# An FNet and feed-forward kernel: the first roots moved from GpSimd to VectorE and ScalarE, and a new table of positions

## The chip, the cores and the metric

The kernel runs on one core of a Trainium2 chip. The metric is the device time of one execution in microseconds. The engines are named as in the profile: PE is TensorE (matmuls; PEld is its weight load), DVE is VectorE, ACT is ScalarE, POOL is GpSimd, and SP is SyncE, which only issues transfers here. POOL issues transfers too.

## The reference

```python
a = jnp.einsum("bsd,ed->bse", x, dft_hid_re)
b = jnp.einsum("bsd,ed->bse", x, dft_hid_im)
y = jnp.einsum("ts,bse->bte", dft_seq_re, a) - jnp.einsum("ts,bse->bte", dft_seq_im, b)
...
h  = x + _A_ref(_layernorm(x), dft_seq_re, dft_seq_im, dft_hid_re, dft_hid_im)
h2 = h + silu(_layernorm(h) @ w1) @ w2
```

x has 2048 rows (S) of 512 columns (D); the sequence matrices are 2048 x 2048, the hidden ones 512 x 512, w1 is 512 x 1792 and w2 1792 x 512. All is fp32.

## The kernel before

**Arithmetic.** Every fp32 operand is split into a rounded high part and a remainder, the low part, and each product is three matmuls (function `three`, L329 to L331: high by high, high by low, low by high). The split takes one pass on ACT (`rounded`, L270; for X and S tiles L421, L449, L456) and one on DVE (L274 or L276, L427). The large products are built by a Strassen-like scheme of seven products (numbers 1 to 7 in the code), so DVE also forms sums and differences of the operands before a product and of the results after it.

**Stages.** `plain(0, 0)` multiplies the normalized x by the first quarter of the sequence matrices while x is still being loaded and normalized; `fast(1, 0)` does the next quarter; `mix_fast(0)` multiplies by the hidden matrices and adds x; then `fast(0, 1)`, `fast(1, 1)` and `mix_fast(1)` do the other half of the output columns; `up` and `down`, twice, are the feed-forward part. Beside them run the normalization of h, the sums of w1, w2 and of the hidden matrices, and stores of half results to DRAM and fetches back.

**Normalizing x.** For each pair of row tiles `stats_x` takes means and variances on DVE (L370, L371); `roots_x` starts the inverse root with a square root on ACT (L291) and computes -var/2; its second half takes a reciprocal on DVE (L298) and does one Newton step and the bias; `norm_x` applies scale and bias on ACT (L403) and rounds (L421); `rest` makes the low parts on DVE (L427). With one column (one row tile) the Newton step and the bias are on DVE (L321, L325, L384) and -var/2 on ACT (L293); with two columns all of that is on POOL (L295, L302 to L305, L386, L387).

**What sets the order.** `program` creates 1598 pieces of work. `step` advances a planned clock by 0.2265 us (`MM_US`) for each matmul and gives each piece before or after it a planned time relative to it; `at` gives a planned time outright. The table `MOVED` then adds a correction to the time of piece n, and the pieces are sorted:

```python
return sorted(((t + MOVED.get(n, 0.0), at, n, f) for t, at, n, f in events), key=lambda v: v[:3])
```

They are issued in that order, and every engine, and every transfer queue, keeps it: an instruction that waits holds up all later ones of its engine. The planned times serve for the order alone; nothing waits for a clock. Most tiles lie in 51 pages of on-chip memory, which are assigned in the same order (`Plan.places`), so a transfer into a page also waits for the last use of what lay there before.

The pieces that the prediction speaks of:

- 5, 11, 12, 14: square root, rest of the root, normalizing and low parts of the second row tile.
- 16, 20, 21: statistics and root; rest of the root and normalizing; low parts, of row tiles 2 and 3 (the rest of the first group of rows).
- 23, 27: roundings of sequence tiles for the steps after that.
- 56, 57 and 102, 103, 104: root, normalizing and low parts of later pairs of row tiles; PE needs 57 for the step near 37 us and 103 for the step near 52 us.
- 72, 112: negated copies of sequence tiles (ACT, L634). 74, 189: roundings for the step near 43 us.
- 62, 115, 142, 158: sums of results of `plain` (DVE, L591, L594).
- 144, 164, 168, 277, 281, 607, 627, 637, 645: remainders (low parts) of sequence tiles; 146, 151: of X tiles; 231, 237: of the hidden matrices.
- 165, 169: transfers on POOL that add a sequence tile to one on chip (L640); 232: a store on POOL.
- 774, 801: fetches of rounded hidden matrices (SP, L854); 919: a fetch of the normalized h; 780, 910, 1001, 1025: loads of x, w2, w1 and w1 (SP); 1002: the rounding of what 1001 loads (ACT, L1074); 951: a copy of a result by ACT (L1104).
- 1267, 1489, 1583, 1587: the last adds and stores of the output (L1251, L1217).

Of the kernel before, what the change touches and what calls it, by code (L numbers as in the profile page):

```python
# [251 lines left out]
def program(nc, page, keep, small, psum, dram, x, xT, seq, hid, ffn, out):  # L252
# [33 lines left out]
    upper = keep.tile([P, 1], F32, name="upper")  # L286
    lower = keep.tile([P, 1], F32, name="lower")

    def rsqrt(var, v, t, q):

        nc.scalar.activation(q, var, AF.Sqrt, scale=1.0, bias=upper)  # L291
        if var.shape[-1] == 1:
# [81 lines left out]
    def roots_x(jj):  # L374

        done, mv, w = stats.pop(jj)
        n = len(done)
# [1044 lines left out]
```

## Time and profile before

| | us |
|---|---|
| median of 3 runs | 674.59 (673.58 to 675.31) |
| the profiled execution | 682.51 |
| its span, first to last instruction | 680.7 |
| PE busy | 664.3 (98%) |
| DVE busy | 574.5 (84%) |
| ACT busy | 374.1 (55%) |
| POOL busy | 123.4 (18%) |

In the groups and the timeline a row has the start, the duration, the engine, the line, the operation, written tile <- read tiles, the shape, and in brackets how long the engine was idle before it and what ended that. In the waits a row has who waited <- for whom, the total, how often, and the longest. In the table of stretches a row has the stretch, its length, the busy time of PE, PEld, DVE, ACT and POOL, the granted PE clock, the share of the transfer engines' time, and GB/s. The profiled execution is 7.9 us longer than the median of the runs.

### The profile page before, as it was taken

Reading aid. Unit: us, or ns where it says so; the run is one execution under the profiler, and the core shown is the slowest. Engines: PE = TensorE matmul, PEld = TensorE weight load, DVE = VectorE, ACT = ScalarE, POOL = GpSimd, SP = SyncE. Lnnn points to the kernel's source line nnn. Section 1 sums busy time; section 2 is a strip of 40 time slices with the busy share of each in tenths; the row PEclk is TensorE's granted clock in tenths of the full one; section 3 lists DMA queues with packets and bytes.
Section 4 is the critical chain, followed back from the end, with each engine's and each line's share of the span. In section 5 each row is a group of like instructions: output and inputs, shape, how many; then the busy total and the mean of one; then the engine's idle time right before and its main releaser. Section 6 shows DMA issues by size and latency. Waiting matters only on the chain.

```text
span 680.7 us, 8334 instructions
## 1 busy us (share of the span) xinstructions
PE 664.3 (98%) x2880; PEld 540.9 (79%) x2880; DVE 574.5 (84%) x714; ACT 374.1 (55%) x479; POOL 123.4 (18%) x183
## 2 busy tenths in 40 slices
PE   8999989999999999999998998999999999999997
PEld 5776868888888888878887886888888888888885
DVE  7888888998989999799999897989999753669774
ACT  5989546655454444446563744668643645655510
POOL 2562211112002331310231003426001000000000
PEclk9999989999999999999999998999999999999999
DMA  9967989999999778999999984787979725468913
GB/s 322 393 119 155 252 291 404 319 282 317 327 314 342 240 213 237 321 372 296 307 352 421 344 286 173 275 300 262 393 215 402 281 83 210 140 224 284 316 40 154
DMA packets 60425, 186.82 MB, mean 274 GB/s; under 512 B 6880, under 2 KB 13920, under 8 KB 60384
## 3 DMA queue, kind: packets, MB, share of 16 engines
q1 hardware_dynamic: 45312, 132.27, 54.8%
q0 software_dynamic: 14784, 53.77, 26.2%
q8 instruction: 22, 0.36, 0.2%
q10 hardware_dynamic: 288, 0.26, 0.1%
q14 instruction: 19, 0.16, 0.1%
HBM read 140.39 MB, written 44.32 MB: 271 GB/s over the span
## 4 chain that ended last, share of the span: by engine, by line
PE 43%; DMA 4%; DVE 3%; ACT 1%; issue 1%; SPq 0%; ACTq 0%; DVEq 0%
PE f L331 6%; PE f L329 6%; PE f L330 6%; PE y L329 5%; PE y L331 5%; PE y L330 5%; PE vx L331 3%; PE vx L329 3%; PE vx L330 3%; DMA hf<-fd 2%; DMA u<-in_ffn 2%; DVE pl L274 1%; DVE raw L742 1%; DVE pl L276 0%; ACT ph L270 0%
## 5 line engine op out<-in xcount | busy, mean ns | idle before, releaser
L270 ACT ACTIVATE ph<-raw 128x1024 fp32r<-128x1024 f32 x98 | 101.3, 1055 | 79.8 <-DVE pl L274 19.3
L274 DVE TENSOR_TENSOR pl<-raw,ph 128x1024 fp32r<-128x1024 f32 x86 | 104.3, 1233 | 15.6 <-ACT ph L270 12.7
L330 PE MATMUL m<-pl,S 128*128 128x512 f32 x192 | 75.2, 392 | 0.2
L331 PE MATMUL m<-ph,S 128*128 128x512 f32 x192 | 74.8, 389 | 0.0
L329 PE MATMUL m<-ph,S 128*128 128x512 f32 x192 | 74.7, 389 | 0.0
L329 PE MATMUL f<-gth,wf 128*128 128x512 f32 x161 | 62.6, 389 | 0.0
L330 PE MATMUL f<-gtl,wf 128*128 128x512 f32 x161 | 62.6, 389 | 0.0
L331 PE MATMUL f<-gth,wf 128*128 128x512 f32 x161 | 62.6, 389 | 0.0
L274 DVE TENSOR_TENSOR gtl<-g,gth 128x1024 fp32r<-128x1024 f32 x42 | 50.4, 1219 | 14.2 <-ACT gth L270 14.2
L270 ACT ACTIVATE gth<-g 128x1024 fp32r<-128x1024 f32 x42 | 42.6, 1053 | 33.1 <-DVE g L1236 17.2
L330 PE MATMUL m<-pl,X 128*128 128x512 f32 x144 | 56.8, 394 | 1.9 <-DVE pl L274 1.8
L329 PE MATMUL m<-ph,X 128*128 128x512 f32 x144 | 56.7, 394 | 0.0
L331 PE MATMUL m<-ph,X 128*128 128x512 f32 x144 | 56.7, 394 | 0.0
L742 DVE TENSOR_TENSOR raw<-raw,raw 128x1024 f32<-128x1024 f32 x36 | 45.8, 1275 | 0.3
L329 PE MATMUL y<-ph,hf 128*128 128x512 f32 x112 | 43.7, 390 | 1.8 <-DMA hf<-fd 1.8
L331 PE MATMUL y<-ph,hf 128*128 128x512 f32 x112 | 43.6, 389 | 0.0
L330 PE MATMUL y<-pl,hf 128*128 128x512 f32 x112 | 43.6, 389 | 0.0
L330 PEld LDWEIGHTS m<-pl,S 128*128 128x128 f32 x192 | 36.0, 188 | 9.3 <-DVE pl L274 1.7
L329 PEld LDWEIGHTS m<-ph,S 128*128 128x128 f32 x192 | 36.0, 188 | 7.5
L331 PEld LDWEIGHTS m<-ph,S 128*128 128x128 f32 x192 | 36.0, 188 | 7.4
L1107 DVE TENSOR_TENSOR g<-vx,g 128x512 f32<-128x512 f32 x28 | 19.3, 689 | 25.8 <-PE vx L331 13.5
L330 PEld LDWEIGHTS f<-gtl,wf 128*128 128x128 f32 x161 | 30.2, 188 | 6.3
(416 smaller groups left out, 1580.5 us busy)
## 6 DMA issues: line engine op xcount, KB each, us to landing
raw<-in_seq SPq DMA_DIRECT2D x83, 512.0 KB, 7.1
hf<-fd SPq DMA_DIRECT2D x28, 512.0 KB, 7.2
wf<-wd SPq DMA_DIRECT2D x28, 512.0 KB, 6.1
wf<-wd SPq DMA_DIRECT2D x28, 384.0 KB, 4.4
sf<-sd SPq DMA_DIRECT2D x18, 512.0 KB, 6.5
raw<-in_seq POOLq DMA_DIRECT2D x15, 512.0 KB, 8.2
fd<-hf POOLq DMA_DIRECT2D x14, 512.0 KB, 7.1
w<-in_ffn SPq DMA_DIRECT2D x23, 256.0 KB, 6.2
```

The lines of the kernel that those rows point to most:

```text
L270: nc.scalar.activation(hi, src, AF.Copy, scale=sign)
L274: nc.vector.tensor_tensor(lo, src, hi, op=ALU.subtract)
L329: nc.tensor.matmul(acc, wh, mh, start=first, stop=False, skip_group_check=on)
L330: nc.tensor.matmul(acc, wh, ml, start=False, stop=False, skip_group_check=on)
L331: nc.tensor.matmul(acc, wl, mh, start=False, stop=last, skip_group_check=on)
L742: nc.vector.tensor_tensor(o, a, b, op=ALU.subtract)
L1107: nc.vector.tensor_tensor(g[q, f][:, tau, :], src, g[q, f][:, tau, :], op=ALU.add)
```

## The change

First, `rsqrt` and `roots_x` no longer choose by the number of columns but by whether the roots belong to a later group of rows (those have a tuple as key). For the first group of rows, whose last two tiles have two columns, -var/2 goes from POOL to ACT, and the Newton step and the bias from POOL to DVE. The other six pairs stay on POOL.

```diff
-    def rsqrt(var, v, t, q):
+    def rsqrt(var, v, t, q, spare=False):
 
         nc.scalar.activation(q, var, AF.Sqrt, scale=1.0, bias=upper)
-        if var.shape[-1] == 1:
+        if not spare:
             nc.scalar.activation(t, var, AF.Identity, scale=-0.5, bias=lower)
         else:
             nc.gpsimd.tensor_scalar(t, var, -0.5, -0.5 * EPS, op0=ALU.mult, op1=ALU.add)
 
         def refine():
             nc.vector.reciprocal(q, q)
-            if var.shape[-1] == 1:
+            if not spare:
                 newton(v, t, q, q)
             else:
                 nc.gpsimd.tensor_tensor(v, q, q, op=ALU.mult)
...
-        refine = rsqrt(mv[:, :n, 1], v, t, r)
+        spare = isinstance(jj, tuple)
+        refine = rsqrt(mv[:, :n, 1], v, t, r, spare)
 
         def then():
             refine()
-            if n == 1:
+            if not spare:
                 nc.vector.scalar_tensor_tensor(b, mv[:, :n, 0], -1.0, r, op0=ALU.mult, op1=ALU.mult)
             else:
                 nc.gpsimd.tensor_tensor(b, mv[:, :n, 0], r, op=ALU.mult)
```

Second, the table `MOVED`: 534 of its 1019 entries have another value and 37 are new. The pieces named above, with the planned time that results (base time plus entry) before and after:

| piece | entry before | after | planned time before | after |
|---|---|---|---|---|
| 5 | -148.22 | -183.24 | -241.1 | -276.1 |
| 11 | -69.54 | -170.43 | -159.7 | -260.6 |
| 12 | -60.5 | -140.25 | -146.4 | -226.2 |
| 14 | -42.39 | -86.88 | -114.2 | -158.7 |
| 16 | -82.56 | -128.07 | -165.6 | -211.1 |
| 20 | -138.51 | -161.4 | -136.6 | -159.5 |
| 21 | -83.19 | -99.75 | -76.3 | -92.8 |
| 23 | -152.04 | -173.57 | -151.4 | -172.9 |
| 27 | -168.5 | -168.5 | -162.4 | -162.4 |
| 57 | -75.05 | -75.05 | -56.9 | -56.9 |
| 72 | -74.26 | -91.97 | -51.6 | -69.3 |
| 112 | -18.19 | -10.85 | 16.3 | 23.6 |
| 189, 74 | -7.95, -5.56 | the same | 19.6, 22.9 | 19.6, 22.9 |
| 115, 62 | 17.99, 18.84 | -0.81, 0.24 | 65.2, 73.7 | 46.4, 55.1 |
| 151, 146 | 3.99, 7.25 | -6.59, -3.29 | 61.2, 61.8 | 50.6, 51.2 |
| 231 | -40.84 | -35.43 | 59.0 | 64.4 |
| 144 | none | none | 59.5 | 59.5 |
| 165, 169 | none, 8.11 | 8.43, 3.17 | 58.4, 69.2 | 66.8, 64.3 |
| 232 | -39.41 | -31.37 | 60.9 | 69.0 |
| 164 | 1.29 | 2.81 | 71.7 | 73.2 |
| 142, 158 | 9.72, 3.24 | 9.72, 6.19 | 74.2, 74.4 | 74.2, 77.4 |
| 281, 277 | 1.14, 5.69 | 3.13, 2.42 | 74.7, 76.5 | 76.7, 73.2 |
| 627, 645 | 4.12, 1.8 | 7.6, 5.04 | 262.5, 268.3 | 266.0, 271.6 |
| 919, 801 | -8.57, -23.53 | -32.05, 4.29 | 341.7, 325.0 | 318.2, 352.8 |
| 774 | -1.69 | -1.69 | 333.2 | 333.2 |
| 780, 910 | 30.22, -25.24 | 20.32, -43.66 | 379.8, 382.0 | 369.9, 363.6 |
| 1001, 1025 | -8.22, -15.73 | -10.97, -55.02 | 382.8, 384.8 | 380.1, 345.6 |
| 1002, 951 | -13.83, none | -6.22, none | 385.0, 387.3 | 392.6, 387.3 |
| 1583, 1587 | 1.39, -0.02 | 49, -0.02 | 644.2, 644.8 | 691.8, 644.8 |
| 1267, 1489 | 106.65, 75.03 | 72.6, 19.98 | 668.1, 707.6 | 634.0, 652.5 |

Piece 607 keeps its place within 0.3 us; other pieces on DVE are moved ahead of it. The order of the matmuls on PE is the same before and after. On DVE about 210 of 542 pieces, on ACT 130 of 444, on SP 56 of 199 and on POOL 20 of 107 stand elsewhere relative to the rest of their queue.

226 rows, old and new, of the table MOVED are left out of this document.

## The prediction

> **What bounds the kernel now.** I read the page's busy shares first, then the waits of PE, then the timeline of PE around the longest of them.
>
> ```profile
> PE 664.3 (98%) x2880; PEld 540.9 (79%) x2880; DVE 574.5 (84%) x714; ACT 374.1 (55%) x479; POOL 123.4 (18%) x183
> ```
>
> PE is busy 98% of the span and the change leaves its instructions and their order alone, so the change can only move waits of PE. These are all of them:
>
> ```profile
> PE y L329 <- ACT g L1104: 2.5, 1, 2.5
> PE c L329 <- ACT X L421: 2.0, 2, 1.1
> PE m L330 <- DVE pl L274: 1.8, 1, 1.8
> PE y L329 <- DMA hf<-fd: 1.8, 1, 1.8
> PE c L541 <- ACT X L403: 1.6, 1, 1.6
> PE idle L1385 <- DVE upper L1378: 1.2, 1, 1.2
> PE c L545 <- DVE X L427: 0.6, 1, 0.6
> ```
>
> Without the start (1.2) they come to 10.3 us; 6.0 of it (2.0, 1.8, 1.6, 0.6) lies in the head, the first 100 us. A wait costs more than its idle time:
>
> ```profile
> 92.97 0.39 PE L329 MATMUL m<-ph,X 128*128 128x512 f32 x1
> 95.18 0.50 PE L330 MATMUL m<-pl,X 128*128 128x512 f32 x1 [1.82 <-DVE pl L274]
> 95.52 0.59 PE L331 MATMUL m<-ph,X 128*128 128x512 f32 x1
> 95.90 0.63 PE L329 MATMUL m<-ph,X 128*128 128x512 f32 x1
> 96.33 0.63 PE L330 MATMUL m<-pl,X 128*128 128x512 f32 x1
> ...
> 92.00:100.00 8.00, 6.18 (x20) 4.61 (x20) 7.12 (x7) 1.69 (x2) 1.59 (x3) 0.79 0.82 242
> 410.00:418.00 8.00, 5.53 (x18) 4.12 (x17) 5.75 (x7) 3.88 (x6) 0.00 (x0) 0.79 0.45 161
> ```
>
> After the wait at 93 the matmuls start 0.43 us apart (95.90 to 96.33) instead of the 0.2265 of the kernel's own MM_US, and the granted clock over these 8 us is 0.79 (the column before the last two): 0.21 x 8 = 1.7 us lost beside the 1.8. The wait that ends in the window 410 to 418 shows the same 0.79. So the wait at 93 is worth 3.5 us, the one at 411 4.2, and all seven about 14.
>
> The Trainium skill, page "TensorE: Matmul & The Clock Gate", section "Why this matters for your kernels", asks only for no idle gaps over about 3 us; by that rule the waits at 93 and 411 would cost their idle time alone, and the forecast below would be 1.7 us higher. Here the trace disagrees: a gap of 1.82 us halved the clock, so I price it at 3.5.
>
> **The change part by part.** The order follows from the code: a piece's planned time plus its entry of the table, sorted. Only the queues of DVE, ACT, POOL and SP change.
>
> *Roots of the first group of rows (pieces 16 and 20).* Seven POOL instructions become one Identity on ACT and four operations on DVE.
>
> ```profile
> 11.06 0.30 ACT L291 ACTIVATE rs<-mv,upper 128x2 f32<-128x2 f32 x1 [1.84 <-DVE rs L298]
> 11.26 1.99 ACT L270 ACTIVATE ph<-raw 128x1024 fp32r<-128x1024 f32 x2
> 13.15 1.08 ACT L403 ACTIVATE X<-x,rs 128x256 fp32r<-128x256 f32 x2
> ...
> 16.42 1.10 ACT L403 ACTIVATE X<-x,rs 128x256 fp32r<-128x256 f32 x2 [1.48 <-POOL rs L387]
> ...
> 37.06 0.63 ACT L421 ACTIVATE X<-xc 128x512 fp32r<-128x512 f32 x1
> 37.60 0.28 ACT L291 ACTIVATE rs<-mv,upper 128x2 f32<-128x2 f32 x1
> 37.78 1.04 ACT L634 ACTIVATE raw<-raw 128x1024 f32<-128x1024 f32 x1
> ```
>
> ```profile
> 46.24 0.55 POOL L302 TENSOR_TENSOR rs<-rs 128x2 f32<-128x2 f32 x1 [1.64 <-DVE rs L298]
> 46.86 1.06 POOL L303 TENSOR_TENSOR rs<-rs 128x2 f32<-128x2 f32 x1
> ...
> 50.88 0.22 POOL L387 TENSOR_SCALAR rs<-rs 128x2 f32<-128x2 f32 x1
> ```
>
> ```profile
> 10.94 0.13 DVE L298 RECIPROCAL rs<-rs 128x1 f32<-128x1 f32 x1
> ...
> 11.64 0.16 DVE L384 SCALAR_TENSOR_TENSOR rs<-mv,rs 128x1 f32<-128x1 f32 x1
> ...
> 72.83 1.22 DVE L274 TENSOR_TENSOR pl<-nb,ph 128x1024 fp32r<-128x1024 f32 x1
> 73.96 0.68 DVE L427 TENSOR_TENSOR X<-xc,X 128x512 fp32r<-128x512 f32 x1
> ...
> 89.18 1.22 DVE L591 TENSOR_TENSOR C<-C,Cp 128x1024 f32<-128x1024 f32 x1
> ```
>
> ACT could begin with these tiles only at 16.42, after 1.48 of waiting for POOL's last instruction. The same work for one tile took DVE 10.94 to 11.80, four instructions in 0.86; with two columns there is one more, so about 1.1. Added: 0.9 on DVE, 0.2 to 0.3 on ACT (the 0.28 row); the roots come about 2.5 us earlier. Left over on POOL: nothing waits there for the time that comes free, so that is worth nothing by itself.
>
> *The head, first wait (1.6).* On ACT, piece 12 (the second row tile, 13.15) stood behind the square root at 11.06, which waits for the statistics of two later tiles, and two roundings (1.99). Now it stands ahead of all three, and its own roots (piece 11) ahead of those statistics on DVE. Its first half is ready near 10.6 instead of 13.7, before PE is done with its first half-step at about 12.0. What is late next are its low parts (piece 14), about 0.5. Worth 1.1 to 1.6, I take 1.5. *Second wait (0.6).* Piece 21 stands ahead of one pair of statistics now, but PE arrives 1.5 earlier: the 0.6 stays.
>
> *Third wait (ACT X L421, the first of two, near 37).* Piece 57 ends at 37.69 in the rows. The 1.04 of piece 72 (37.78) moves from behind it to ahead of it; what ACT idled for earlier POOL roots in this stretch is saved in exchange. I put its end at 36.9 to 37.1. PE comes 1.5 earlier, so its wait grows from 0.9 to about 1.6, and only 0.7 of the gain is left here. This is the step at which most of the first gain is lost.
>
> *Fourth wait (the second of two, near 52).* Piece 103 needs the POOL chain of 46.24 to 51.10. Its reciprocal comes earlier by about 2 us, because pieces 72 and 112 (1.04 each on ACT) no longer stand between 57 and the pair 189 and 74, on which DVE's queue waits. If the chain keeps its 4.9 us, it ends near 49.2, ACT is done at 51.4, and PE gets there at 51.3: no wait. Gain so far about 2; bounds 0 (the chain starts no earlier) and 3.
>
> *DVE between 55 and 76.* Pieces 115 and 62 (1.22 each, the L591 row) and 151 and 146 (0.68 each) come forward by 10 to 19 us of plan: 3.8 us of work that no PE step needs yet, ahead of the remainder 144 (72.83). With the 0.9 of the roots that is 4.7; DVE had waits in this stretch that take up the rest, 231 (0.68) moves behind, and I put 144's end at 75.6 for 74.05. PE, counted back from 92.97 by six steps of 2.72, came for it near 76.3 before; 2 us earlier it finds it missing and waits about 1.4. Gain left: 0.8 to 1.3.
>
> *Fifth wait (93).* Here the rows are:
>
> ```profile
> 86.30 2.36 DVE L274 TENSOR_TENSOR pl<-raw,ph 128x1024 fp32r<-128x1024 f32 x2 [3.50 <-ACT ph L270]
> ...
> 92.77 2.35 DVE L274 TENSOR_TENSOR pl<-raw,ph 128x1024 fp32r<-128x1024 f32 x2
> ```
>
> DVE stood idle 3.5 us until 86.30 (a POOL transfer, piece 169, was late) and then did the remainder 237, three sums (62, 142, 158) and the remainder 281 before 277, the second of the pair at 92.77, which ended at 95.12 and which PE waits for. Now 169 is issued ahead of 165 and 232, the sums 62 and 115 are done long before, and 277 stands ahead of 142, 158 and 281. It ends near 87 to 90; PE comes near 92. The wait and its half clock go: 3.5. Cover: at least 2 us of DVE's lead; without it the 1.8 returns.
>
> Head in sum: 1.5 - 0.8 (lost at the third wait) + 1.3 (fourth) - 0.9 (DVE) + 3.5 (fifth) = 4.6. Ends: 0 and 8.
>
> *From 100 to 320.* No PE wait over the bound of the view. Some remainders come later by 3 to 4 us of DVE work (607, 645, also 627 and 637 by 1.2 to 2.4), which is more than the 1 to 3 us that stood between them and PE. I take 1.0 lost; between 0 and 3.5 (the 3.5 of one full wait with half clock).
>
> *The middle (369 and 411).* The hf transfers keep about the same bytes ahead of the late one (801 goes behind it, 919 comes ahead, 0.5 MB each): 1.8 stays. At 411, ACT's copy L1104 stood behind a rounding that waits for piece 1001's transfer. That rounding (1002) now stands behind the copy (951), and pieces 780, 910 and 1025, which shared the queue with the transfer, are issued 10 to 39 us of plan earlier. Late next is 1002 itself, which PE needs one step (1.4) after the copy; if the transfer comes earlier by about that much, the whole 4.2 goes in a run that has this wait.
>
> *The end.* The adds and two stores of 1583 change places with 1587, 1267 and 1489 in the last 10 us; PE's last matmuls cover them, bound plus or minus 0.5, taken as 0. *Page reuse:* 51 pages are assigned anew; each assignment keeps the planned order of uses, taken as 0, and its bound lies in the rivals.
>
> *Sum.* The profiled execution took 682.51 (its span and the 1.8 around it stand in the table above), 7.9 above the median of 674.59, so the timed runs lack more than half of the 14 us of waits. The two of the middle hang on transfers, which vary; the head's hang on fixed work. In the profile: 682.5 - 4.6 + 1.0 - 4.2 = 674.7. In the runs: 674.6 - 4.6 + 1.0 = 671.0, and a quarter of the 4.2, since some runs may hold that wait: 670.0.
>
> **The rivals.** *All waits of the middle are in the timed runs too.* Then 674.6 - 4.6 - 4.2 + 1.0 = 666.8. For it: the change attacks them. Against it: 7.9 us between profile and runs must be something.
>
> *The head's gain is absorbed.* The six root chains left on POOL decide the third and fourth wait. Their length swings: a 128x2 instruction took 0.22 at 50.88 and 1.06 at 46.86. If DVE's denser queue makes the earlier ones as long as the 4.9 us at 46, pieces 57 and 103 come no earlier, gains up to there are zero, and the 0.9 on DVE remains: 674.6 - 3.5 + 0.9 + 1.0 = 673.0, no change. The Trainium skill, page "SBUF — State Buffer", section "Who interferes with whom", states that a DVE instruction with two SBUF inputs contends with a GpSimd one that reads SBUF, the loser blocked for the whole instruction. By that rule this rival is the outcome; the trace agrees with the rule (0.22 against 1.06), and leaves open how often it strikes in the new order.
>
> *Slower: DVE becomes the bound between 66 and 92.* If DVE reclaims none of its idle time, the 3.1 us by which 144 moves, and the 2.4 of 164, fall on PE: 144 would end at 77.2 for 76.3, 164 at 90.0 for 87.6, and the second wait brings a half clock: 0.9 + 2.4 + 1.7 = 5.0 lost, against 3.5 won at 93; with two such waits of 1.0 and 1.2 more at 270 to 295 it is 674.6 + 1.5 + 2.2 = 678.3. It decides once DVE reclaims less than about 2 us. For it: DVE is the second busiest engine (84%). Against it: the 3.5 us idle at 86 shows that there is room.
>
> **How the numbers follow.** Forecast as summed, between 667.5 and 672.5: 0.48. Middle too: 0.17. Absorbed: 0.16. Slower: 0.19. The bound of 0.3%, which is what this measurement can tell from no change, is 2.0 us: faster below 672.6, slower above 676.6. Faster: 0.48 + 0.17 + a fifth of the absorbed = 0.68; same 0.13; slower 0.19. Range: 664 (the middle's rival with a better head) to 678 (the slower one's price), 8 in 10.
>
> **What would show it.** PE's wait on ACT X L403 gone; one longer wait on ACT X L421 near 36 and none near 50; a new wait of about 1.4 on DVE pl near 74; no wait and full clock at 90 to 98; no wait on ACT g L1104. POOL without roots before 17 us. Wrong if new PE waits with a clock of 0.8 stand between 260 and 320, or if POOL's roots of 40 to 50 us still end at 51.

## The result, and the profile after

| | before | after |
|---|---|---|
| median of 19 runs, us | 677.33 (673.58 to 681.3) | 670.0 (668.18 to 674.45) |
| ratio | | 0.9894 (0.9873 to 0.9914) |
| profiled execution, us | 682.51 | 669.66 |
| its span, us | 680.7 | 667.9 |
| mean granted clock of PE in it | 0.994 | 1.000 |

The changed kernel is 1.06% faster, 7.2 us of 677.33 (5.8 to 8.6 by the interval). The time is the one that was predicted, but it was reached from another start: the median of 674.59 from which the sum began came from three runs, and 19 runs put it 2.7 us higher. The gain was predicted 2.6 us too small, and the two errors cancel by luck. For the profiled execution the same sum gave 674.7; it took 669.66, 5.0 less.

First the busy line of the page of the changed kernel, then its waits of PE (who waited for whom, total, times, longest):

```profile
PE 658.9 (99%) x2880; PEld 539.1 (81%) x2880; DVE 573.7 (86%) x718; ACT 376.3 (56%) x480; POOL 123.6 (19%) x176
```

```profile
PE idle L1390 <- DVE upper L1383: 1.2, 1, 1.2
PE c L333 <- ACT X L426: 1.1, 1, 1.1
PE c L550 <- DVE X L432: 1.0, 2, 0.6
PE c L334 <- DVE pl L278: 0.5, 1, 0.5
PE m L334 <- DVE pl L278: 0.3, 1, 0.3
PE y L333 <- ACT u L716: 0.3, 1, 0.3
```

Without the start, 3.2 us of waits are left of 10.3, and none is longer than 1.1. The matmul behind the wait at 93 starts at 90.11 now (95.18 before), the one behind the wait at 411 at 402.08 (413.26 before). The stretches around them (the clock is the third column from the right):

```profile
84.00:92.00 8.00, 7.50 (x34) 6.19 (x34) 8.00 (x9) 4.09 (x6) 1.07 (x2) 1.00 1.02 402
398.00:406.00 8.00, 8.00 (x37) 6.63 (x36) 7.96 (x9) 3.84 (x6) 2.31 (x1) 1.00 0.82 313
```

Both have the full clock (0.79 before). To see where the time went I took, from PE's timeline of both kernels, the distance from each matmul's start to the next one's, less the 0.2265 us of an undisturbed one, and summed it by stretches of each kernel's own clock:

```
us          6-18  18-30  30-45  45-66  66-90  90-100  100-320  320-340  340-380  380-420
before      2.14   0.90   1.48   2.67   0.46    3.73     1.15     0.40     2.51     4.27
after       1.26   1.01   1.65   0.07   0.85    0.01     0.39     0.02     1.91     0.03
predicted   -1.5    0     +0.8   -1.3   +0.9    -3.5     +1.0              0       -4.2
measured    -0.9   +0.1   +0.2   -2.6   +0.4    -3.7     -0.8     -0.4     -0.6     -4.2
```

These make 12.5 us; with 0.4 at the two ends that is the 12.9 by which the profiled executions differ. The runs differ by 7.2: the profiled execution of before is longer than any of its 19 runs, that of the changed kernel lies at its median.

### The profile page after: what moved, and what is told of

It is laid out like the page before. It is cut to its first block, busy times and chain, and to the rows that moved or that the text cites. A ratio compares the mean times of both kernels' runs of the same rounds, so it can differ in the third digit from the quotient of the medians.

```text
span 667.9 us, 8303 instructions
## 1 busy us (share of the span) xinstructions
PE 658.9 (99%) x2880; PEld 539.1 (81%) x2880; DVE 573.7 (86%) x718; ACT 376.3 (56%) x480; POOL 123.6 (19%) x176
## 4 chain that ended last, share of the span: by engine, by line
PE 75%; DMA 7%; DVE 3%; issue 3%; POOL 1%; ACT 0%; SPq 0%; POOLq 0%; DVEq 0%; ACTq 0%
PE m L334 8%; PE m L335 8%; PE m L333 8%; PE y L334 8%; PE y L335 7%; PE y L333 7%; PE f L334 6%; PE f L335 6%; PE f L333 6%; DMA raw<-in_seq 3%; PE vx L335 3%; PE vx L334 3%; PE vx L333 3%; DMA w<-in_ffn 2%; DMA wd<-Vl 1%
## 5 line engine op out<-in xcount | busy, mean ns | idle before, releaser
L333 PE MATMUL m<-ph,S 128*128 128x512 f32 x192 | 74.7, 389 | 0.0
L335 PE MATMUL m<-ph,S 128*128 128x512 f32 x192 | 74.7, 389 | 0.0
L334 PE MATMUL m<-pl,S 128*128 128x512 f32 x192 | 74.7, 389 | 0.0
L333 PE MATMUL m<-ph,X 128*128 128x512 f32 x144 | 56.0, 389 | 0.0
L335 PE MATMUL m<-ph,X 128*128 128x512 f32 x144 | 56.0, 389 | 0.0
L333 PEld LDWEIGHTS f<-gth,wf 128*128 128x128 f32 x161 | 30.2, 188 | 6.3
```

The lines of the kernel that those rows point to most:

```text
L333: nc.tensor.matmul(acc, wh, mh, start=first, stop=False, skip_group_check=on)
L334: nc.tensor.matmul(acc, wh, ml, start=False, stop=False, skip_group_check=on)
L335: nc.tensor.matmul(acc, wl, mh, start=False, stop=last, skip_group_check=on)
```

## The experiments

In the experiments the rewritten table has a few lines more or fewer, so line numbers move by up to five against the changed kernel; operations and tile names stay. Table entries are the corrections in us. Each run's kernel before was run on the same chip.

**Head and rest.** The changes in two complementary parts, cut at pieces that started before and after 122 us.

```diff
 # head: roots, and the 145 entries of pieces that started before 122 us
-    11: -69.54, 12: -60.5, 277: 5.69, 62: 18.84, 115: 17.99,
+    11: -170.43, 12: -140.25, 277: 2.42, 62: 0.24, 115: -0.81,
 ...
 # rest: the other 426 entries
-    801: -23.53, 919: -8.57, 1002: -13.83, 1025: -15.73,
+    801: 4.29, 919: -32.05, 1002: -6.22, 1025: -55.02,
 ...
```

> Roots and table entries of the pieces that started before 122 us; all later pieces stand where they stood before. Theory A (the head's waits hang on fixed work and are in every run, the middle's are in a few): almost the whole gain, 6 to 7 us under the kernel before, ratio 0.990 to 0.991; waits of PE at 37, 52 and 93 as in the changed kernel, and the waits near 369 and 411 still there in the profile. Theory B (the middle's waits are in most runs, and the head gives only the 2 to 3 us that they leave of the 7.3): ratio 0.995 to 0.997.

> The complement of the head: roots as before, the new table entries for the pieces from 122 us on alone. Theory A: 0 to 1.5 us faster, ratio 0.998 to 1.000, with the waits of the first 100 us unchanged in the profile. Theory B: 4 to 5 us faster, ratio 0.993 to 0.994. If the two parts do not add up to the whole (the ratios of head and rest multiplied come out more than 0.003 away from 0.989), they share a wait.

Head: 672.87 (670.43 to 678.18), ratio 0.9934 (0.9906 to 0.9961). Rest: 678.03 (676.91 to 680.28), ratio 1.0013 (0.9992 to 1.0033). The waits of head, then of rest, the later stages' rows:

```profile
PE y L333 <- DMA hf<-fd: 3.0, 1, 3.0
PE y L333 <- ACT g L1109: 1.7, 1, 1.7
```

```profile
PE m L336 <- DVE pl L280: 2.6, 2, 1.8
PE m L335 <- ACT p L717: 1.1, 1, 1.1
PE y L335 <- ACT u L717: 1.0, 1, 1.0
```

Head alone brings about 4.5 us, between what the two theories said; rest alone brings nothing; the product of the ratios, 0.9947, is 0.0053 above that of the whole. So the parts are not independent. In head the two waits of the middle are there, 4.7 us together. In rest they are gone (2.1 us of lost distance between 340 and 420, for 6.8 in the profiled execution of before), but beside the old waits of the head stand new ones of 1.1 at 140, 0.8 at 286 and 1.0 at 366.

**Roots alone, order alone.** The two kinds of edit of the change, each without the other.

```diff
 # roots: code of after, table of before
-        refine = rsqrt(mv[:, :n, 1], v, t, r)
+        spare = isinstance(jj, tuple)
+        refine = rsqrt(mv[:, :n, 1], v, t, r, spare)
 # order: code of before, table of after
```

> The code of the changed kernel (first group's roots on ACT and DVE), with the table of before, entry for entry. Theory A (the order carries the head's gain; the roots only make room for it): the wait of PE on ACT X at 12 to 14 stays, since piece 12 still stands behind the square root and the roundings; ratio 0.998 to 1.001. Rival (the roots themselves carry the head's 4.7 us): ratio 0.993 to 0.995, and the waits at 37 and 52 go.

> The code of before (the first group's roots on POOL, seven instructions), with the table of the changed kernel, entry for entry. Theory A: ACT waits 1.5 to 2.5 us for POOL at 12 to 15, PE's wait near 20 grows by 1 to 2 us, nearly all else as in the changed kernel; ratio 0.990 to 0.993. Rival (roots and order need each other): the gain up to 66 us is gone, ratio 0.994 to 0.997.

Roots: 674.65 (671.98 to 680.5), ratio 0.9984 (0.9958 to 1.001). Order: 669.33 (667.62 to 670.51, 6 runs), ratio 0.9891 (0.9864 to 0.9918). In roots the first, the fourth and the fifth wait (1.9, at 93) stand (the third, near 37, is gone, one of the two that the rival named):

```profile
PE c L544 <- ACT X L406: 1.9, 1, 1.9
PE c L331 <- ACT X L424: 1.1, 1, 1.1
```

In order, POOL's chain for the first group's last roots starts at 13.60 and has its last instruction at 15.21; ACT, which needs it, waits 0.33, where 1.5 to 2.5 was expected, and PE's wait near 20 stays at 0.4:

```profile
13.60 0.29 POOL L309 TENSOR_TENSOR rs<-rs 128x2 f32<-128x2 f32 x1 [0.71 <-DVE rs L305]
...
15.21 0.24 POOL L394 TENSOR_SCALAR rs<-rs 128x2 f32<-128x2 f32 x1
```

```profile
15.48 1.09 ACT L410 ACTIVATE X<-x,rs 128x256 fp32r<-128x256 f32 x2 [0.33 <-POOL rs L394]
```

The table carries the whole gain. With the pieces in their new places this POOL chain takes 1.85 us; in the kernel before the same chain took 3.8 (12.57 to 16.38). There two of its instructions took 1.06 and 1.09, beside two remainders on DVE (12.99 to 15.34); in order DVE has short low parts (0.74 from 13.43) and then statistics (from 14.49), and none of the chain takes more than 0.29. So the roots' move is worth nothing that these runs can tell.

**The middle put back.** The changed kernel with the entries from 306 to 415 us as before.

```diff
-    801: 4.29, 919: -32.05, 1002: -6.22,
+    801: -23.53, 919: -8.57, 1002: -13.83,
 ...
```

> The changed kernel, with the 111 entries of the pieces that started between 306 and 415 us put back. Theory A: 0 to 1.5 us slower than the changed kernel, ratio to the kernel before 0.990 to 0.992. Theory B: 4 to 5 us slower than the changed kernel, ratio 0.995 to 0.997, and the wait of PE on ACT's copy near 400 (the 411 of before, less the head's gain) in the profile, with a half clock behind it.

674.4 (673.31 to 675.74), ratio 0.9955 (0.9935 to 0.9975), 4.4 us over the changed kernel. But the waits are not the ones expected:

```profile
PE m L337 <- DVE pl L281: 2.2, 2, 1.7
```

The 2.2 lie at 316 and 320, at the seam of the two orders, and no row on ACT g is there. Theory B's number came out by another cause. The rounding stands ahead of the copy again, but its load (piece 1001) took only 6.3 us from issue to landing (396.5 to 402.9), and the copy was done before PE came for it at 404.5:

```profile
402.94 0.85 ACT L1082 ACTIVATE wah<-w 128x768 fp32r<-128x768 f32 x1 [1.76 <-DMA w<-in_ffn]
403.69 0.58 ACT L1112 ACTIVATE g<-y 128x512 f32<-128x512 f32 x1
```

So the order of the two makes the wait possible, and the time of the load decides whether it comes.

**The five entries of the wait at 411**, added to the kernel before, taken out of the changed kernel, and added to head.

```diff
-    1001: -8.22, 1002: -13.83, 780: 30.22, 910: -25.24, 1025: -15.73,
+    1001: -10.97, 1002: -6.22, 780: 20.32, 910: -43.66, 1025: -55.02,
```

> The kernel before, with only five entries changed: 1001, 1002, 780, 910 and 1025 (the rounding behind ACT's copy, and the transfers that shared a queue with its source). If these five are the cause of the wait at 411: no wait of PE on ACT g near 411, clock 1.00 between 410 and 418, and 4.2 us less in a run that had the wait. Theory A: ratio 0.998 to 1.000 over the runs. Theory B: 0.993 to 0.995. Rival: the wait is not theirs (other entries between 306 and 415 are needed), then it stays and the ratio is 1.000.

> The changed kernel, with the same five entries put back (1001, 1002, 780, 910, 1025). With the five alone the kernel before gained only 0.9 us of its 677.6, ratio 0.9991 (0.9969 to 1.0012). Theory A (the wait at 411 is in a quarter of the runs): 0.5 to 1.5 us slower than the changed kernel, ratio to the kernel before 0.990 to 0.992. Theory B (once the head is out of the way the transfers of the middle decide in every run): 3 to 4.5 us slower than the changed kernel, ratio 0.994 to 0.996, wait on ACT g near 400 in the profile.

> Roots and the entries of the first 122 us, as in head, and of all later entries only the five of the wait at 411 (1001, 1002, 780, 910, 1025). Theory C (the waits of the middle hang on transfers that do not come forward as far as PE does, so that they take back part of what the head gains): the 2.9 us that head (672.9) lacks to the changed kernel (670.0) come from these five: 670 to 671, ratio 0.989 to 0.991. If parts just add up: 672.9 less the 0.9 that the five gave alone, 672.0, ratio 0.992. If the five only work in company of the other later entries: 673 or more, ratio 0.994.

Added to before: 676.65 (673.5 to 678.61), ratio 0.9991 (0.9969 to 1.0012). Taken out of after: 676.48 (674.33 to 679.47), ratio 1.000 (0.998 to 1.002). Added to head: 672.36 (669.78 to 679.16), ratio 0.9928 (0.9901 to 0.9955). ACT's timeline shows the two instructions in the kernel before, in the kernel before with the five, in the changed kernel, and in the changed kernel without the five:

```profile
411.88 0.84 ACT L1074 ACTIVATE wah<-w 128x768 fp32r<-128x768 f32 x1 [4.55 <-DMA w<-in_ffn]
412.63 0.58 ACT L1104 ACTIVATE g<-y 128x512 f32<-128x512 f32 x1
```

```profile
408.75 0.60 ACT L1106 ACTIVATE g<-y 128x512 f32<-128x512 f32 x1 [2.14 <-PE y L333]
...
413.04 0.85 ACT L1076 ACTIVATE wah<-w 128x768 fp32r<-128x768 f32 x1
```

```profile
400.92 0.60 ACT L1109 ACTIVATE g<-y 128x512 f32<-128x512 f32 x1 [2.14 <-PE y L335]
...
404.13 0.84 ACT L1079 ACTIVATE wah<-w 128x768 fp32r<-128x768 f32 x1
```

```profile
407.00 0.84 ACT L1082 ACTIVATE wah<-w 128x768 fp32r<-128x768 f32 x1 [7.06 <-DMA u<-in_ffn]
407.75 0.58 ACT L1112 ACTIVATE g<-y 128x512 f32<-128x512 f32 x1
```

Before, the rounding `wah` holds the copy `g` back until its load has landed. With the five added the load lands as late as before (412.0, before 411.8), but the copy goes when PE has its result, and no wait of PE on ACT g is left; in the changed kernel it is the same, with the rounding 3.2 us behind the copy. That is the mechanism that the prediction named, and it is shown from both sides: without the five the wait is back, as PE's longest:

```profile
PE y L336 <- ACT g L1112: 3.1, 1, 3.1
```

The sizes are the lesson. In the kernel before, the five are worth 0.6 us (a gain of 2.1 to a loss of 0.8 by the interval); in its profile the wait on the fetch `hf` is longer instead (2.7 for 1.8), with a half clock behind it. In the changed kernel they are worth 6.5 by the medians and 7.2 by the ratios, the whole gain; every one of its 12 runs without the five had a mean clock of 0.997 or less. There PE's last matmul ahead of the wait started at 404.87 instead of 410.40, 5.5 earlier, while the load (piece 1001) landed at 406.9 instead of 411.8, 4.9 earlier (the row names a load of u, but that landed only at 408.9): it went out at 395.3, behind 910 at 392.6, and took 11.6 us, where in the changed kernel it goes out at 390.0 and takes 6.9. By the lost distances, PE in this profile is 7.3 us ahead of before at 380, and 4.9 ahead once the wait is over, so 2.5 of the gain goes here. In the runs nothing of it is left; what takes the rest is not shown, and the profile of before is 5 us longer than its median run. Theory C for head was still wrong in its choice: the five added to head leave 672.4. The profiled execution of that kernel, one of its longest, has no wait on ACT g, but

```profile
PE y L333 <- DMA hf<-fd: 3.2, 1, 3.2
PE y L335 <- DVE wal L432: 1.7, 1, 1.7
```

The wait on the fetch `hf` at 361 is the one that stays in head and in head with the five, and that the changed kernel lacks. That its entries are the missing ones was not tried alone.

**The wait at 93**, alone and together with the five.

```diff
-    169: 8.11, 277: 5.69, 281: 1.14, 62: 18.84, 158: 3.24, 115: 17.99,
+    169: 3.17, 277: 2.42, 281: 3.13, 62: 0.24, 158: 6.19, 115: -0.81,
```

> The kernel before, with six entries changed: 169, 277, 281, 62, 158 and 115 (the transfer that was late, the remainder that PE waited for at 93, and the sums around it). If these are the cause: no wait of PE on DVE pl at 90 to 98, clock 1.00 there, 3.5 us less where the half clock was. The single-run profiles so far show that wait with 1.84 and half clock in one kernel and with 0.77 and none in another, so over the runs I expect 1.5 to 3 us, ratio 0.9955 to 0.998. Rival: the remainder is late anyway, ratio 1.000, and the wait stands at 90 to 96.

> The kernel before with eleven entries: the six of the wait at 93 (alone 1.0009) and the five of the wait at 411 (alone 0.9991). If parts add up: ratio 1.000. Theory C (the gain at 93 was taken back at 367 and 411): 2 to 3 us faster, ratio 0.9955 to 0.997. Rival (the gain at 93 was lost again at once, in the wait of 0.97 that came up at 77): ratio 0.998 to 1.000, with that wait in the profile and none at 411.

Alone: 677.09 (675.64 to 680.89), ratio 1.0009 (0.9982 to 1.0036). With the five: 676.03 (674.93 to 677.89), ratio 0.9983 (0.9956 to 1.001). The wait at 93 is gone in both (0.02 and 0.04 us of lost distance from 90 to 100). The waits of the first, then of the second:

```profile
PE y L331 <- DMA hf<-fd: 2.0, 1, 2.0
...
PE y L331 <- ACT g L1106: 1.3, 1, 1.3
...
PE c L333 <- DVE X L429: 1.0, 1, 1.0
```

```profile
PE c L333 <- DVE X L429: 0.9, 1, 0.9
```

A wait of 1.0 on DVE X came up at 77: the sums 62 and 115 are drawn ahead of it, and the remainder 144 ends at 76.7 and 77.4 instead of 74.05. In the changed kernel other pieces' moves make up for that. Of the 3.5 that the wait at 93 was priced at, 2.5 would be left, and in a run in which it brought no half clock (see the last section), 0.8. Alone, the interval allows a gain of 1.2 at most, so it holds the 0.8 and not the 2.5; with the five it holds both; both hold zero. That the middle takes the rest back is not settled by them, since combo's median falls to the rival's side of the line drawn beforehand.

**The sums back.** The changed kernel, with three pieces of DVE where they stood.

```diff
-    115: -0.81, 62: 0.24, 151: -6.59,
+    115: 17.99, 62: 18.84, 151: 3.99,
```

> The changed kernel with three entries put back: 115, 62 and 151, 3.1 us of VectorE work that the change drew ahead by 10 to 22 us. By the prediction's step on VectorE (0.9 lost near 74 because of them): the wait of PE on DVE pl at 83.6 (0.5 to 0.8) goes, 0.3 to 0.9 us faster than the changed kernel, ratio 0.988 to 0.989. Rival (they had to leave the stretch ahead of the remainder 277): a wait on DVE pl of 1 to 2 us at 85 to 92, 1 to 3.5 us slower, ratio 0.991 to 0.995.

672.51 (671.14 to 675.28), ratio 0.9932 (0.9908 to 0.9956), 2.5 us over the changed kernel: the rival. Its waits, and DVE's timeline:

```profile
PE c L337 <- DVE pl L281: 1.3, 1, 1.3
...
PE c L338 <- DVE S L435: 1.1, 1, 1.1
```

```profile
66.95 0.69 DVE L838 TENSOR_TENSOR hs<-hid,hid 128x512 f32<-128x512 f32 x1 [1.03 <-PE c L337]
...
72.44 1.23 DVE L281 TENSOR_TENSOR pl<-nb,ph 128x1024 fp32r<-128x1024 f32 x1 [1.74 <-ACT ph L277]
...
77.15 1.21 DVE L602 TENSOR_TENSOR C<-C,c 128x1024 f32<-128x1024 f32 x1
78.28 1.22 DVE L281 TENSOR_TENSOR pl<-nb,ph 128x1024 fp32r<-128x1024 f32 x1
```

Without the sums DVE idles 1.03 and 1.74 there, and does one of them (77.15) right ahead of the remainder that PE then waits 1.3 for. In the changed kernel they fill that idle time and cost nothing.

**Two steps more by the same means.** ACT's timeline of the changed kernel has the pattern of 411 once more: a rounding waits 6.80 for its load, and two copies behind it, whose sources PE finished at 349, are late for the step at 357.

```profile
355.85 0.85 ACT L1079 ACTIVATE wah<-w 128x768 fp32r<-128x768 f32 x1 [6.80 <-DMA w<-in_ffn]
356.60 1.07 ACT L716 ACTIVATE u<-m 128x512 f32<-128x512 f32 x2
```

```diff
-        spare = isinstance(jj, tuple)
+        spare = isinstance(jj, tuple) and jj != (3, 1)
-    57: -75.05, 978: -50.1, 979: -47.08,
+    57: -76.6, 978: -43.7, 979: -45.2,
```

> The changed kernel and two steps more by the same means. First, the roots of one later pair of tiles (row group 3, second pair) go to ACT and DVE too, and piece 57 stands ahead of the 1.04 us of piece 94 on ACT: the wait of PE on ACT X near 36 (1.1) should fall to under 0.2. Second, piece 978, a rounding that keeps ACT idle for 6.8 us until a transfer lands, stands behind 740, for which PE waits at 357, and 979 moves with it: that wait (0.3 to 1.2) and the 0.5 at 361 should go. Theory C: the first gain comes through only if the middle lets it: 668.0 to 669.0, ratio 0.9865 to 0.988. Rival (VectorE's added work or the later release of the page under 978 costs as much): 670, ratio 0.989, with a longer wait on DVE pl near 83 or on a transfer near 370.

668.38 (667.27 to 668.95, 6 runs), ratio 0.9866 (0.9833 to 0.9898). The waits on ACT X near 36 and on ACT u at 357 are gone; the copies run at 348.64, and the longest wait but the start's is

```profile
PE m L337 <- DVE pl L281: 0.8, 1, 0.8
```

```profile
348.64 1.09 ACT L719 ACTIVATE u<-m 128x512 f32<-128x512 f32 x2 [0.21 <-PE m L337]
```

It is the fastest kernel of all by its median. Against the changed kernel it is 1.6 us lower, as expected, which the intervals (0.0033 wide to each side) cannot tell from none; that both waits went is shown.

## Why the prediction was right, and where its terms were wrong

**What bounds the kernel** held: PE's instructions stayed, and the gain is waits of PE that went. The absorbed and the slower rival did not happen. The third rival, that the waits of the middle are in the timed runs too, did in part: the 2.9 us that head alone lacks to the whole lie in the runs.

**First wait** (predicted -1.5, measured -0.9 in the profile). Piece 12 now starts on ACT at 10.39, as the order said, ahead of the square root at 12.08; PE does not wait there. What is late next is a low part, as the step said, though of the tile before: a wait of 0.6 on DVE X at 8.2, which is why 0.6 of the 1.5 did not come. The second wait stayed, as said (0.6 before, 0.4 now).

**Third wait** (+0.8, +0.2). Piece 57 ended at 36.86, and 36.9 to 37.1 was said. The rows of ACT show it, right behind the end of its POOL chain (34.64):

```profile
34.67 1.52 ACT L408 ACTIVATE xc<-x,rs 128x512 f32<-128x512 f32 x2
36.23 0.63 ACT L426 ACTIVATE X<-xc 128x512 fp32r<-128x512 f32 x1
```

PE came only 1.0 earlier, so its wait grew from 0.9 to 1.1, not to 1.6.

**Fourth wait** (-1.3, -2.6). The POOL chain was said to end near 49.2; it ended at 48.25 and piece 103 at 50.47 instead of 53.31. The whole wait went.

**DVE from 55 to 76** (+0.9, +0.4) is the step of the head that failed. For the work drawn forward it put the end of the remainder 144 at 75.6, 1.55 later than before. The stretch did grow by that: from the start of the low part 104 to the end of 144 it took 20.7 us before and 22.3 now. But DVE, too, had waited for piece 103 in the kernel before, and this the step left out:

```profile
53.34 0.69 DVE L427 TENSOR_TENSOR X<-xc,X 128x512 fp32r<-128x512 f32 x1 [2.60 <-ACT X L421]
```

```profile
50.50 0.69 DVE L432 TENSOR_TENSOR X<-xc,X 128x512 fp32r<-128x512 f32 x1 [0.88 <-ACT X L426]
```

So the stretch began 2.84 earlier, and 144 ended at 72.76, 1.3 earlier than before. Where it does not begin earlier (the wait at 93 alone, 53.75), 144 ended at 76.7, and PE did wait 1.0. With the earlier start, the sums fill idle time of DVE further on; putting three pieces back costs 2.5. The small wait that is there (0.5, at 84.0) belongs to the remainder 164, which ended at 84.47.

**Fifth wait** (-3.5, -3.7). The first of these rows of DVE holds the pieces 164 and 277, the last piece 281, behind them as said:

```profile
83.24 2.36 DVE L278 TENSOR_TENSOR pl<-raw,ph 128x1024 fp32r<-128x1024 f32 x2 [2.00 <-ACT ph L274]
...
87.25 1.22 DVE L278 TENSOR_TENSOR pl<-raw,ph 128x1024 fp32r<-128x1024 f32 x1
```

Piece 277 ended at 85.6, where 87 to 90 was said. For the profiled execution the price was right. For the runs it was too high: the half clock in it comes in only some of them (see the last section).

**From 100 to 320** (+1.0, -0.8). The loss did not come in the profile of the changed kernel. In those of order, sums back, two steps more and the changed kernel without the five, which have the same entries here, a wait of 0.5 to 0.8 on a remainder stands between 278 and 281, and the stretch loses 1.3 to 1.7 (1.15 before); in rest, where the head was old, waits of 1.1 and 0.8 came. So there the term is 0.2 to 0.5, not 1.0.

**The wait at 369** (0, -0.6). The step said that it stays, because 801 goes behind the late fetch (774) and 919 comes ahead of it, 0.5 MB each. This was wrong: 919 goes out at 327.2 and has landed at 338.9, before 774 goes out at 346.5, so it is not ahead of 774 in any way that counts. 774 went out 8.3 earlier than before and took 14.3 us for 14.9, so it landed at 360.7 instead of 369.6, 8.9 earlier, while PE came 7.1 earlier. In head, where 919 goes out right behind 774, at 349.7, it took 16.3. That one transfer less beside it is the reason was not tried alone. The wait on the fetch, 1.8, went, and smaller ones at 346, 357 and 361 stand in its place.

**The wait at 411** (-4.2 in the profile, a quarter of it in the runs). Its mechanism is shown by the five entries. In the profile the term was right to 0.1, and in the kernel before the five are worth 0.6 us in the runs, near the 1.05 taken. But the step treated the middle as a term to be added, and it is not: without the five, the head's gain did not reach the end of the runs (ratio 1.000). The head's sum (4.6) measured 6.5 in the profile, 4.5 in the runs of head alone, and 7.2 with the middle repaired. So the mis-sized terms are the fourth wait (1.3 too little), DVE, the stretch from 100 to 320, the wait at 369, and the one left out: how the two repairs help each other.

Open is why rest alone gives nothing in the runs. In its profile, the stretch from 100 to 320, with two of the new waits, loses 1.9 us more than before, and a half clock behind the wait at 14, which the profile of before lacks, costs 2.3; but no run took these away.

## What to carry to other kernels

Where an engine keeps its order, look for instructions that wait for a transfer ahead of ones that PE needs: the copy behind such a rounding was the costliest wait, and the same pattern gave the next step. A wait's price is not its own: one that hangs on transfers can eat what is won before it (the same five entries were worth 0.6 us in one kernel and 6.5 in the other), so repairs are to be tested together and not only one by one. And work that is drawn forward on a busy engine costs nothing if it lands in that engine's idle time, which its timeline shows.

## What the runs showed of the hardware

The half clock goes by a fixed grid, not by the length of a wait. In the 14 profiles 12 stretches at half clock lie amid the work; each lasts 3.41 us, and each starts a whole number of 3.41 us after the first record of the clock (the phase differs from run to run). In 11 of the 12, PE was idle for 51% or more of the 3.41 us ahead (in the twelfth for 47%), and of all other such intervals of the grid none was idle for more than 49% but one (56%, below). The stretches are: before, the wait at 93 and the stretch behind it; before, the wait at 368, nearly as long, which falls on two intervals; head, the one exception.

```profile
92.15:95.56 3.41, 1.59 (x8) 1.00 (x7) 3.41 (x4) 0.00 (x0) 0.00 (x0) 1.00 0.63 208
95.56:98.97 3.41, 3.41 (x10) 2.65 (x9) 3.41 (x4) 1.06 (x1) 1.05 (x2) 0.50 1.07 299
365.20:368.62 3.42, 2.67 (x12) 1.88 (x10) 3.28 (x4) 1.15 (x2) 0.00 (x0) 1.00 1.02 419
368.62:372.03 3.41, 2.34 (x10) 1.96 (x11) 3.38 (x4) 0.00 (x0) 0.00 (x0) 1.00 1.03 423
```

```profile
358.88:362.29 3.41, 1.51 (x7) 0.93 (x5) 3.31 (x4) 0.00 (x0) 0.00 (x0) 1.00 1.03 423
362.29:365.70 3.41, 2.30 (x10) 1.91 (x11) 3.38 (x4) 0.00 (x0) 0.00 (x0) 1.00 1.02 416
```

The first wait, 1.82, leaves PE 1.59 busy of 3.41 and halves the next interval; the other, 1.82 too, is split and halves none. If an interval that is idle for half of its time, 1.7 us, halves the next, a single wait under 1.7 us costs only itself (two of 1.67 did, though the one of 1.60 in the twelfth case did not), and one of 1.8 costs 1.8 or 3.5 as the phase falls: by such a grid 3.5 in 1.82 of 3.41 cases, 53%, which makes it 2.7 on the mean, an estimate from these rows. The kernel before shows the spread: of 93 runs 29 had a mean clock of 0.999 or more (median 676.0), 44 of 0.996 to 0.998 (677.4), and 20 of 0.995 or less (679.5), where one half interval takes 0.5 x 3.41 / 676 = 0.0025 from the mean. The changed kernel has 15 of 19 at 0.999 or more.

The Trainium skill, page "TensorE: Matmul & The Clock Gate", section "Part 1: The HAM clock gate", speaks of a free-running window of 4096 cycles, about 3.4 us; the runs agree with it (3.41 on a grid). That a gap has to be over about 3 us, as the page's section "Why this matters for your kernels" has it, the runs contradict: ten waits of 1.6 to 2.7 us were each followed by a halved stretch.
